# A planned instruction order that counts longer landing times for transfers and a shorter hop from TensorE

## The chip, the cores and the metric

The kernel runs on one core of a Trainium2 chip. The metric is the device time of one execution in microseconds (us); the times below are the median of the runs and their range. The core has five engines. Four matter here: TensorE (PE, matrix products), VectorE (DVE) and ScalarE (ACT, both elementwise work), and SyncE (SP), whose queue issues the transfers (DMAs). Each engine runs its own list of instructions in the order in which it was written, and waits on semaphores for the others.

## The reference

Attention over channels, then two feed-forward layers, on 6016 tokens of 256 channels:

```python
qn = q / (norm(q, axis=1) + 1e-6);  kn = k / (norm(k, axis=1) + 1e-6)
a = softmax(kn.T @ qn / tau)                    # 256 x 256
x = v @ a                                       # 6016 x 256
xn = x / sqrt(mean(x * x, -1) + 1e-6) * rms_g
y = (silu(xn @ w_gate) * (xn @ w_val)) @ w_out  # d_ff 1536
h = y @ w_in2
out = (h - tanh(h)) @ w_out2                    # d_ff 2048
```

## The kernel before

Everything is in fp32 accuracy: each operand of a large product is split into a high part (made by ACT, names ending in `h`) and a low part (made by DVE, names ending in `l`), and one product is three matmuls (`prod`, line 399). Activations are held transposed, channels on partitions, in blocks of 512 tokens. Two blocks make a pair, and there are six pairs; the first is smaller.

The work comes in stages. First the attention matrix, from `q` and `k`, while the weights of the first layer are loaded and converted (`convert`, nine blocks `items`, in the order `gv0`, `w10`, `gv1`, `gv2`, ...). Then pair 0 of the first layer, in plain form. Then pairs 1 to 5 of the first layer: a product of two blocks of weights by two blocks of channels and tokens is done by a scheme with seven products in place of eight (`unit`), on four PSUM banks X, T, Y, Z; its operands B11, B21, B22 and T1 to T4 are parts of the blocks, their sums and differences, which `operands` makes. Each of the six units of a pair is a gate part (tiles `Xg`, `Yg`, ...) and a value part (`Xv`, ...; in `value_sum` DVE makes the sum `c`), and its four results are split (`uc`, `ulc`) and pushed as products into four accumulator banks (`acc`). When an accumulator is full, ACT copies it to `r`, a ring of one buffer (`rr`), and `to_y` writes it to memory. Last come the six pairs of the second layer, eight units each (tiles `Xh`, `Yh`, `Zh`, `Th`; results `wc`), whose sums go out as `outT`.

While a pair of the first layer runs, `x_thread` (line 874) prepares the next one: it multiplies `v` by the attention matrix, then sends the mean squares through memory to turn them (transfers `row`, then `narmp`), takes the inverse root on DVE, writes it (`back`), and reads it spread over all partitions (`rs`, 256 KB each); DVE multiplies `x_0g` and `x_1g` by `rs`, and `operands` follows. Beside it `second_weights` converts the weights of the second layer: load `raw` (512 KB), convert on ACT and DVE to `y`, write it (`l<-y`, `l20s<-y`, ..., 256 KB).

The order of all of this is not that of the program text. Each operation is put into a graph with an engine, a cost, and what it reads and writes (`Graph.op`). `Graph.run` (line 149) is a list scheduler: it plays the four engines in time, and gives each, when it is free, the ready operation of lowest rank. PE ranks by a key, the place of the operation in the program (accumulations get a lag); the others rank by `late`, the latest start that `Graph.latest` (line 226) found by going backward over the last round's order. An operation is ready when the ends of what it depends on, plus a hop between the two engines (`LATENCY`, line 24), have passed. The end of a transfer is counted by its issue, its bytes and a tail (line 33 and lines 189 to 193):

```python
DMA_SETUP, DMA_RATE, DMA_TAIL, DMA_ISSUE = 1000, 385.0, 900, 450
...
                free[e] = t + DMA_ISSUE
                wire = max(t + DMA_SETUP, wire) + o.size / DMA_RATE
                o.end = wire + DMA_TAIL
```

`Graph.schedule` plays six rounds, keeps the order with the earliest end, and the instructions are written in it. The planned times have no other effect: on the chip an instruction waits for its data alone, and those behind it on its engine wait with it.

Of the kernel before, what the change touches and what calls it, by code (L numbers as in the profile page):

```python
# [21 lines left out]


LATENCY = {
    ("PE", "PE"): 0, ("PE", "ACT"): 262, ("PE", "DVE"): 262,
    ("ACT", "PE"): 152, ("DVE", "PE"): 140, ("DVE", "ACT"): 120, ("ACT", "DVE"): 132,
    ("ACT", "ACT"): 130, ("DVE", "DVE"): 116,
    ("SP", "SP"): 100, ("SP", "PE"): 100, ("SP", "ACT"): 100, ("SP", "DVE"): 100,
# [2 lines left out]
COLD = 7000.0  # L31
PATIENT, HOLD, TOLERANCE = ("ACT", "DVE"), 600.0, 60.0
DMA_SETUP, DMA_RATE, DMA_TAIL, DMA_ISSUE = 1000, 385.0, 900, 450


class Op:
    __slots__ = ("eng", "cost", "emit", "preds", "succs", "key", "idx", "start", "end", "late",
                 "ready", "left", "size")

    def __init__(self, eng, cost, emit, key, idx, size):  # L40
        self.eng, self.cost, self.emit, self.key, self.idx, self.size = (
            eng, cost, emit, key, idx, size)
        self.preds, self.succs, self.late = {}, [], None


class Part:
# [42 lines left out]
class View:  # L89
# [5 lines left out]
    @property  # L95
    def ap(self):
        return self.f(self.buf.t)
# [14 lines left out]
class Graph:  # L112
# [36 lines left out]
    def run(self):  # L149

        ops = self.ops
        for o in ops:
            o.left, o.ready = len(o.preds), 0.0
        free = dict.fromkeys(("PE", "ACT", "DVE", "SP"), 0.0)
        known = {e: [] for e in free}
        avail = {e: [] for e in free}
        wire = lag = 0.0

        def rank(o):
            return (o.key if o.eng == "PE" else o.idx if o.late is None else o.late, o.idx)  # L160

        for o in ops:
            if not o.left:
                heappush(known[o.eng], (0.0, o.idx))
        order = []
        while len(order) < len(ops):
            best = None
            for e in free:
                if avail[e]:
                    t = free[e]  # L170
                elif known[e]:
                    t = max(free[e], known[e][0][0])
                else:
                    continue
                if best is None or t < best[0]:
                    best = t, e
            t, e = best
            while known[e] and known[e][0][0] <= t:
                o = ops[heappop(known[e])[1]]
                heappush(avail[e], (*rank(o), o))  # L180
            o = heappop(avail[e])[2]
            if e in PATIENT and o.late is not None:
                o = self.patient(o, t, known[e], avail[e], ops, lag)
                if not isinstance(o, Op):
                    free[e] = o
                    continue
            o.start = t
            if e == "PE" and o.late is not None:
                lag = t - o.late
            if e == "SP":  # L190
                free[e] = t + DMA_ISSUE
                wire = max(t + DMA_SETUP, wire) + o.size / DMA_RATE
                o.end = wire + DMA_TAIL
            else:
                o.end = free[e] = t + o.cost * (2 if e == "PE" and t < COLD else 1)
            order.append(o)
            for s, data in o.succs:
                s.left -= 1
                s.ready = max(s.ready, o.end + self.gap(o, s, data))
                if not s.left:  # L200
                    heappush(known[s.eng], (s.ready, s.idx))
        return order
# [23 lines left out]
    def latest(self, order):  # L226

        end = max(o.end for o in order)
        after = None
        for o in reversed(order):  # L230
            late = end
            for s, data in o.succs:
                late = min(late, s.late - self.gap(o, s, data))
            if o.eng == "PE":
                if after is not None:
                    late = min(late, after.late)
                after = o
            o.late = late - (DMA_SETUP + o.size / DMA_RATE + DMA_TAIL if o.eng == "SP" else o.cost)

    def schedule(self, rounds):  # L240
        for o in self.ops:
# [32 lines left out]
def attn_moe_kernel(  # L274
# [40 lines left out]
    late = []  # L315

    g = Graph()
    slots, early_users = {}, []
# [71 lines left out]
    def lo_of(out, in_, hi, n):  # L390
        return dve(
            lambda: nc.vector.tensor_sub(out=ap(out), in0=ap(in_), in1=f32(ap(hi))), n, 2,  # L392
            [in_, hi], [out])

    def dma(out, in_, size, reads=(), writes=()):
        return g.op(
            "SP", DMA_ISSUE, lambda: nc.sync.dma_start(out=ap(out), in_=ap(in_)), reads, writes,
            size=size)

    def prod(out, w, x, n, start, key=None):  # L400

        (wh, wl), (xh, xl) = w, x

        def emit():
            o = ap(out)
            for i, (a, b) in enumerate(((wh, xh), (wl, xh), (wh, xl))):
                nc.tensor.matmul(  # L407
                    o, ap(a), ap(b), start=start and i == 0, stop=i == 2, skip_group_check=True)

        return g.op("PE", 3 * (n / 2.4 + 13.7), emit, [wh, wl, xh, xl], [out], key=key)  # L410
# [73 lines left out]
    items = []  # L484
# [27 lines left out]
    def convert(c):  # L512

        raw = raws(f"{c['nm']}raw")
        share = W // len(c["src"])
        for s, src in enumerate(c["src"]):
            part = raw.part(s)
            dma(raw.view(lambda t, s=s: t[:, s * share:(s + 1) * share, :].rearrange(
                "p (k n) w -> p k (n w)", k=c["rows"])), src, W * P * 8 // len(c["src"]),
                writes=[part])  # L520
        every = list(raw.parts.values())
        y = ys(f"{c['nm']}y")

        def reads(f):
            before = len(g.ops)
            f()
            o = g.ops[before]
            for p in every:
                for w in p.w:
                    o.preds[w] = True  # L530
                p.r.append(o)
                p.buf.users.append(o)

        reads(lambda: rebias(y, raw, W))
        shift(y, W)
        reads(lambda: sign(y, words(raw, 1), W))
        reads(lambda: bits(y, words(raw, 0), W))
        if "saved" in c:
            dma(c["saved"], y, W * P * 4, [y], [c["saved"]])
        h, l = (new(wpool, f"{c['nm']}{x}", f"{c['nm']}{x}", [P, W], F32R) for x in "hl")  # L540
        both = ["S", "R"]
        activation(h, y, AF.Copy, W, writes=[h.part(x) for x in both])
        dve(lambda: nc.vector.tensor_sub(out=ap(l), in0=ap(y), in1=f32(ap(h))), W, 2,
            [y, *(h.part(x) for x in both)], [l.part(x) for x in both])
        c["h"], c["l"] = h, l
# [39 lines left out]
    def first_sums(i):  # L585
        c = gv[i]
        y = new(act, "wraw", f"s{i}", [P, 2, 4 * P])
        dma(y, c["saved"].view(lambda t: t.rearrange("p (x n) -> p x n", x=2)), W * P * 4,
            [c["saved"]], [y])
        block_sums(y, 2 * P)  # L590
        sh, sl = (new_late(f"s{x}{i}", f"s{x}{i}", [P, 2, 3 * P]) for x in "hl")

        def two(b, key=None):
            return b.view(lambda t: t.rearrange("p (x n) -> p x n", x=2)[:, :, :P], key)

        hi_of(sh, y[:, :, P:], 6 * P)
        hi_of(two(c["h"], "S"), y[:, :, :P], 2 * P)
        lo_of(sl, y[:, :, P:], sh, 6 * P)
        lo_of(two(c["l"], "S"), y[:, :, :P], two(c["h"], "S"), 2 * P)
        for x in range(2):  # L600
            def half(b, key):
                return b
            unit1[i][x] = seven_first(c["h"], c["l"], sh, sl, x)
# [515 lines left out]


    attention()
    for c in items:
        convert(c)
    early_users += [o for b in g.ops for o in [b]]

    xs = [[bank(tag, f"x{b}_{c}") for c, tag in enumerate(tags)]
          for b, tags in enumerate((WORK[:2], WORK[2:]))]
# [193 lines left out]
```

## Time and profile before

| | us |
|---|---|
| median of 3 runs | 1144.27 |
| range of the runs | 1143.41 to 1145.62 |
| the profiled execution, its own time | 1147.1 |
| its span, first to last instruction | 1145.3 |
| PE busy | 1125.6 (98%) |
| DVE busy | 817.5 (71%) |
| ACT busy | 694.0 (61%) |
| mean granted clock of PE | 0.995 |

The profile is of one execution. An engine's busy time is the union of its instructions' times; matmuls are pipelined and their ends modelled, so a busy PE is not PE at its peak. The granted clock is the share of PE's full clock. In the rows further down, `Yv<-T4h,gv4h` reads: writes tile Yv from T4h and gv4h, with buffer numbers left out. What stands behind `<-` in square brackets is what ended the idle time in front of that instruction. Where an instruction waits for several things, the profile names the one that came last.

### The profile page before, as it was taken

How to read it: one execution, taken by the hardware profiler on the slowest of the kernel's cores; microseconds unless marked ns; L12 is line 12 of the kernel's file. 1: busy time of each engine (PE TensorE's matmuls, PEld its weight loads, DVE VectorE, ACT ScalarE, POOL GpSimd, SP SyncE). 2: the span in 40 equal slices, each digit the busy share in tenths (PEclk: the TensorE clock that was granted, in tenths of full speed). 3: DMA queues.
4: the chain of work that ended last, by engine and by line, in shares of the span. 5: the costliest groups of instructions: out<-in, count | busy, mean ns of one | idle time of the engine just before them, and what ended most of it. 6: DMA issues, size and time to landing. Idle time of an engine off the chain costs nothing.

```text
span 1145.3 us, 14185 instructions
## 1 busy us (share of the span) xinstructions
PE 1125.6 (98%) x4986; PEld 927.1 (81%) x4986; DVE 817.5 (71%) x1376; ACT 694.0 (61%) x1199; POOL 0.7 (0%) x6
## 2 busy tenths in 40 slices
PE   9899999999999999999999999999999999999998
PEld 8668887777777887888788899888888888888887
DVE  5988777687678557645966786866867767767664
ACT  6665456665655565555665675756756656656654
POOL 0000000000000000000000000000000000000000
PEclk9999999999999999999999999999999999999999
DMA  9845112422331300010121210200200100100001
GB/s 362 304 149 182 56 64 89 120 84 92 100 107 52 120 20 19 28 42 20 42 88 52 72 54 1 70 1 3 72 1 28 47 1 28 38 1 1 37 1 37
DMA packets 41195, 76.74 MB, mean 67 GB/s; under 512 B 6810, under 2 KB 11674, under 8 KB 41124
## 3 DMA queue, kind: packets, MB, share of 16 engines
q1 hardware_dynamic: 40836, 74.79, 19.6%
q10 hardware_dynamic: 288, 1.05, 0.2%
q8 instruction: 39, 0.64, 0.2%
q14 instruction: 32, 0.26, 0.1%
HBM read 54.02 MB, written 21.80 MB: 66 GB/s over the span
## 4 chain that ended last, share of the span: by engine, by line
PE 76%; DVE 11%; DMA 8%; ACT 3%; issue 2%; SPq 0%; DVEq 0%; ACTq 0%
PE acc L407 33%; PE Yh L407 8%; PE Xh L407 6%; PE Yv L407 4%; PE Yg L407 4%; PE Zh L407 3%; PE Th L407 3%; PE Xg L407 3%; PE Xv L407 2%; DMA rs<-back 2%; PE g L407 2%; PE v L407 2%; DVE tc L388 2%; DVE ulc L392 1%; DMA raw<-w_out_in 1%
## 5 line engine op out<-in xcount | busy, mean ns | idle before, releaser
L392 DVE TENSOR_TENSOR ulc<-wc,uc 128x512 fp32r<-128x512 f32 (+1 forms) x192 | 130.2, 679 | 83.8 <-ACT uc L373 81.4
L373 ACT ACTIVATE uc<-wc 128x512 fp32r<-128x512 f32 (+1 forms) x192 | 119.5, 623 | 103.2 <-PE acc L407 91.4
L373 ACT ACTIVATE uc<-tc 128x512 fp32r<-128x512 f32 x120 | 73.4, 628 | 81.4 <-DVE tc L388 81.0
L392 DVE TENSOR_TENSOR ulc<-tc,uc 128x512 fp32r<-128x512 f32 x120 | 78.5, 683 | 2.7 <-ACT uc L373 2.4
L388 DVE TENSOR_TENSOR Zv<-Yv,m5v 128x512 f32<-128x512 f32 x30 | 20.9, 695 | 40.8 <-PE Yv L407 40.7
L388 DVE TENSOR_TENSOR wc<-Xh,wc 128x512 f32<-128x512 f32 (+1 forms) x48 | 32.5, 676 | 18.6 <-ACT wc L373 18.6
L388 DVE TENSOR_TENSOR Zh<-Yh,m5h 128x512 f32<-128x512 f32 (+1 forms) x48 | 32.9, 686 | 17.9 <-ACT m5h L373 16.0
L373 ACT ACTIVATE wc<-Xh 128x512 f32<-128x512 f32 (+1 forms) x48 | 28.2, 587 | 28.7 <-PE Xh L407 28.5
L415 PE MATMUL S<-q,k 128*128 128x256 f32 x188 | 41.8, 381 | 0.5 <-DMA k<-k_in 0.4
L415 PEld LDWEIGHTS S<-q,k 128*128 128x128 f32 x188 | 35.3, 190 | 6.0 <-issue 1.3
L388 DVE TENSOR_TENSOR wc<-Yh,wc 128x512 f32<-128x512 f32 (+1 forms) x48 | 32.6, 678 | 10.3 <-ACT wc L373 10.3
L373 ACT ACTIVATE wc<-Yh 128x512 f32<-128x512 f32 (+1 forms) x48 | 28.2, 586 | 15.2 <-PE Yh L407 14.5
L373 ACT ACTIVATE r<-acc 128x512 f32<-128x512 f32 (+2 forms) x48 | 27.3, 587 | 15.8 <-PE acc L407 11.3
L373 ACT ACTIVATE m5h<-Th 128x512 f32<-128x512 f32 (+1 forms) x48 | 28.2, 588 | 11.5 <-PE Th L407 11.5
L373 ACT ACTIVATE tc<-Xg 128x512 f32<-128x512 f32 x30 | 17.9, 598 | 27.9 <-PE Xg L407 27.7
L373 ACT ACTIVATE Yh<-Xh 128x512 f32<-128x512 f32 (+1 forms) x48 | 27.6, 575 | 11.7 <-PE Xh L407 10.3
L373 ACT ACTIVATE tc<-Zg 128x512 f32<-128x512 f32 x30 | 17.9, 597 | 25.7 <-PE Zg L407 20.2
L388 DVE TENSOR_TENSOR s<-Yh,m5h 128x512 f32<-128x512 f32 (+1 forms) x48 | 32.5, 676 | 0.3 <-PE Yh L407 0.2
L388 DVE TENSOR_TENSOR wc<-s,wc 128x512 f32<-128x512 f32 (+1 forms) x48 | 32.3, 672 | 0.1
L388 DVE TENSOR_TENSOR wc<-Zh,wc 128x512 f32<-128x512 f32 (+1 forms) x48 | 32.2, 672 | 0.0
L388 DVE TENSOR_TENSOR tc<-Yg,m5g 128x512 f32<-128x512 f32 x30 | 20.7, 690 | 16.0 <-PE Yg L407 15.6
L407 PE MATMUL acc<-uc,w11h 128*128 128x512 f32 x80 | 31.4, 393 | 0.0
(911 smaller groups left out, 3496.9 us busy)
## 6 DMA issues: line engine op xcount, KB each, us to landing
q<-q_in SPq DMA_DIRECT2D x11, 512.0 KB, 8.8
vraw<-vT_in SPq DMA_DIRECT2D x11, 512.0 KB, 4.2
y<-r SPq DMA_DIRECT2D x22, 256.0 KB, 2.2
y<-y SPq DMA_DIRECT2D x20, 256.0 KB, 2.6
outT<-r SPq DMA_DIRECT2D x20, 256.0 KB, 2.0
k<-k_in SPq DMA_DIRECT2D x9, 512.0 KB, 10.3
raw<-w_in_in SPq DMA_DIRECT2D x8, 512.0 KB, 4.4
raw<-w_out_in SPq DMA_DIRECT2D x8, 512.0 KB, 3.8
```

The lines of the kernel that those rows point to most:

```text
L373: nc.scalar.activation(out=ap(out), in_=ap(in_), func=func, **{x: ap(a) for x, a in kw.items()})
L388: return dve(lambda: f(out=ap(out), in0=ap(a), in1=ap(b)), n, 2, [a, b], [out])
L392: lambda: nc.vector.tensor_sub(out=ap(out), in0=ap(in_), in1=f32(ap(hi))), n, 2,
L407: nc.tensor.matmul(o, ap(a), ap(b), start=start and i == 0, stop=i == 2, skip_group_check=True)
L415: lambda: nc.tensor.matmul(ap(out), ap(a), ap(b), start=start, stop=stop, **kw),
```

## The change

Three things are changed, all in the planner. The hop from PE to ACT is counted as 210 ns in place of 262, and that from PE to DVE as 205. Each operation has a new field `slack`, added to the counted end of a transfer and taken off its latest start. Transfers get a slack of 2200 ns from the fourth weight block on (`i > 2`) and in all that follows; those of the attention part and of the first three blocks get none. The line with `early_users` is only written differently.

```diff
 LATENCY = {
-    ("PE", "PE"): 0, ("PE", "ACT"): 262, ("PE", "DVE"): 262,
+    ("PE", "PE"): 0, ("PE", "ACT"): 210, ("PE", "DVE"): 205,
...
 DMA_SETUP, DMA_RATE, DMA_TAIL, DMA_ISSUE = 1000, 385.0, 900, 450
+DMA_SLACK = 2200
...
-        self.preds, self.succs, self.late = {}, [], None
+        self.preds, self.succs, self.late, self.slack = {}, [], None, 0
...
-                o.end = wire + DMA_TAIL
+                o.end = wire + DMA_TAIL + o.slack
...
-            o.late = late - (DMA_SETUP + o.size / DMA_RATE + DMA_TAIL if o.eng == "SP" else o.cost)
+            o.late = late - (DMA_SETUP + o.size / DMA_RATE + DMA_TAIL + o.slack if o.eng == "SP" else o.cost)
...
+    slack = [0]
+
     def dma(out, in_, size, reads=(), writes=()):
-        return g.op(
+        o = g.op(
             "SP", DMA_ISSUE, lambda: nc.sync.dma_start(out=ap(out), in_=ap(in_)), reads, writes,
             size=size)
+        o.slack = slack[0]
+        return o
...
     attention()
-    for c in items:
+    for i, c in enumerate(items):
+        slack[0] = DMA_SLACK if i > 2 else 0
         convert(c)
-    early_users += [o for b in g.ops for o in [b]]
+    early_users += g.ops
+    slack[0] = DMA_SLACK
```

## Rows read from the trace of the kernel before

**Rows 1.** The page's first part: busy us, share of span, instructions of each engine.

```profile
PE 1125.6 (98%) x4986; PEld 927.1 (81%) x4986; DVE 817.5 (71%) x1376; ACT 694.0 (61%) x1199; POOL 0.7 (0%) x6
```

**Rows 2.** Windows: stretch, length, busy us of each engine, clock, DMA share, GB/s.

```profile
140.00:675.00 535.00, 526.33 (x2299) 427.38 (x2298) 379.23 (x669) 316.28 (x563) 0.00 (x0) 1.00 0.21 67
675.00:1145.30 470.30, 466.52 (x2084) 390.27 (x2083) 329.48 (x510) 294.71 (x517) 0.00 (x0) 1.00 0.07 23
```

**Rows 3.** Waits of PE in 140 to 560 us: total us, times, longest us.

```profile
PE Yv L407 <- DVE c L388: 5.2, 4, 2.4
PE Yg L407 <- ACT Yg L373: 0.7, 1, 0.7
...
```

**Rows 4.** Timeline of PE: start us, us, instruction, [idle before <- what ended it].

```profile
246.07 0.50 PE L407 MATMUL Yv<-T4h,gv4h 128*128 128x512 f32 x1 [1.41 <-DVE c L388]
...
348.95 0.50 PE L407 MATMUL Yv<-T4h,gv4h 128*128 128x512 f32 x1 [2.43 <-DVE c L388]
```

**Rows 5.** Timeline of DVE ahead of those two stalls of PE.

```profile
243.52 0.69 DVE L388 TENSOR_TENSOR x_0g<-x_0g,rs 128x512 f32<-128x512 f32 x1 [1.53 <-DMA rs<-back]
...
345.55 0.69 DVE L388 TENSOR_TENSOR x_0g<-x_0g,rs 128x512 f32<-128x512 f32 x1 [1.70 <-DMA rs<-back]
...
347.60 0.69 DVE L388 TENSOR_TENSOR x_0g<-x_0g,rs 128x512 f32<-128x512 f32 x1 [0.76 <-DMA rs<-back]
348.21 0.68 DVE L388 TENSOR_TENSOR c<-Yv,m5v 128x512 f32<-128x512 f32 x1
```

**Rows 6.** Waits of DVE and ACT on transfers, 140 to 560 us, as rows 3.

```profile
DVE x_0g L388 <- DMA rs<-back: 14.9, 6, 4.9
...
ACT y L373 <- DMA raw<-w_out_in: 7.7, 6, 3.1
...
ACT r L373 <- DMA y<-r: 3.1, 4, 1.6
...
DVE y L388 <- DMA l<-y: 3.1, 2, 1.6
```

**Rows 7.** DMA issues: transfer, queue, count, KB each, median us from issue to landing.

```profile
y<-r SPq DMA_DIRECT2D x22, 256.0 KB, 2.2
...
raw<-w_in_in SPq DMA_DIRECT2D x8, 512.0 KB, 4.4
...
l<-y SPq DMA_DIRECT2D x16, 256.0 KB, 4.2
rs<-back SPq DMA_DIRECT2D x10, 256.0 KB, 4.1
```

**Rows 8.** A window, as rows 2, just behind the stall that ends at 348.95.

```profile
350.00:354.00 4.00, 4.00 (x13) 3.15 (x12) 3.48 (x7) 3.12 (x6) 0.00 (x0) 0.61 0.01 3
```

**Rows 9.** Timelines of PE and ACT in the second layer, as rows 4.

```profile
849.06 0.39 PE L407 MATMUL Xh<-B11l,l24h 128*128 128x512 f32 x1
849.29 0.39 PE L407 MATMUL acc<-uc,l22h 128*128 128x512 f32 x1
...
849.49 0.58 ACT L373 ACTIVATE Yh<-Xh 128x512 f32<-128x512 f32 x1 [0.28 <-PE Xh L407]
...
851.10 0.39 PE L407 MATMUL Th<-T1l,l2s 128*128 128x512 f32 x1
...
851.59 0.60 ACT L373 ACTIVATE m5h<-Th 128x512 f32<-128x512 f32 x1 [0.34 <-PE Th L407]
```

**Rows 10.** Timeline of ACT: the first and the last of four copies r.

```profile
573.94 0.60 ACT L373 ACTIVATE r<-acc 128x512 f32<-128x512 f32 x1 [2.81 <-PE acc L407]
...
585.17 0.60 ACT L373 ACTIVATE r<-acc 128x512 f32<-128x512 f32 x1 [0.56 <-DMA y<-r]
```

**Rows 11.** A window as rows 2, and timelines of DVE and PE around T4.

```profile
545.00:563.00 18.00, 17.94 (x78) 14.01 (x77) 17.64 (x30) 12.32 (x22) 0.00 (x0) 1.00 0.19 52
...
563.16 0.68 DVE L392 TENSOR_TENSOR T4l<-t,T4h 128x512 fp32r<-128x512 f32 x1
...
568.97 0.39 PE L407 MATMUL Yg<-T4h,gv0h 128*128 128x512 f32 x1
```

More of the change, by code (lines that the diff above doesn't have):

```diff
@@ L33 @@
 DMA_SETUP, DMA_RATE, DMA_TAIL, DMA_ISSUE = 1000, 385.0, 900, 450
+DMA_SLACK = 2200
 class Op:
     __slots__ = ("eng", "cost", "emit", "preds", "succs", "key", "idx", "start", "end", "late",
-                 "ready", "left", "size")
+                 "ready", "left", "size", "slack")
     def __init__(self, eng, cost, emit, key, idx, size):
```

## The prediction

> **What bounds the kernel now.** I read the busy line first. TensorE (PE) is busy 1125.6 of 1145.3 us [rows 1], and none of its products is added or taken away, so all that an order can win lies in the 19.7 us in which it is idle and in time at a low clock. The windows by stage say where that is. From 675 us on PE is busy 466.52 of 470.30 us, and the missing 3.78 us are the tail behind its last product: nothing to win there, only to lose [rows 2]. In 140 to 675 us, the five block pairs of the first layer, it is busy 526.33 of 535 us: 8.67 us idle [rows 2].
>
> Who ends these waits? The table of PE's waits names VectorE (DVE) and ScalarE (ACT), led by the sum `c` in DVE with 5.2 us in 4 waits [rows 3]. No row names a DMA, and it would be wrong to stop there. The two longest, 1.41 us at 246.07 and 2.43 us at 348.95, end with a `c` on DVE [rows 4]. In DVE's own order the `c` of 348.21 stands right behind `x_0g<-x_0g,rs`, for which DVE sat idle 1.70 us and then 0.76 us until the transfer `rs<-back` landed; the stall at 246.07 has the same wait, 1.53 us, ahead of it [rows 5]. So a short instruction that needs late data stands in the written order ahead of one that PE needs. The waits of DVE and ACT on transfers in 140 to 560 us are of this kind: 14.9 us for `rs`, 7.7 us for `raw`, 3.1 us for `y<-r`, 3.1 us for `l<-y` [rows 6].
>
> The planner's own numbers explain it. It counts 1000 + bytes/385 + 900 ns from issue to landing: for 256 KB 1000 + 681 + 900 = 2581 ns, for 512 KB 3262 ns. The profile has 4.1 us for `rs`, 4.2 us for `l<-y` (both 256 KB), 4.4 us for `raw` (512 KB), but 2.2 us for `y<-r` (256 KB) [rows 7]. Three of the four land 1.1 to 1.6 us after the plan has their readers start; the fourth lands early.
>
> After the stall near 349 us the granted clock over 350 to 354 us is 0.61 [rows 8]. Those 4 us did the work of 4 x 0.61 = 2.44 us at the full level, 2.4 GHz; the rest was spent at 1.2 GHz, and 1.56 us were lost.
>
> **The change, part by part.** *Longer landings.* Every transfer from the fourth weight block's load on is counted 2200 ns longer: 256 KB takes 4781 ns in the plan, 512 KB 5462 ns. Both are above the medians of `rs`, `l<-y` and `raw` [rows 7]. The readers then stand behind other work of their engine, and the wait in front of `c` goes. No instruction is added; what moves is the place of the readers (10 products `x_0g`, 10 `x_1g`, the splits behind them, the conversions of the second layer's weights), and of the transfers on the SP queue, which go out earlier where the plan now counts a chain as longer. Worth: all 8.67 us [rows 2] if every stall of 140 to 675 us has such a transfer behind it, plus the 1.56 us of clock [rows 8], together 10.2 us. The lower end is nothing, if the readers keep their places. I take the upper end less 1.2 us. The rows show the cause for the two longest stalls alone, 3.84 us with the clock loss beside it [rows 4, 8]; for the rest I go by 28.8 us of engine waits on transfers, 14.9 + 7.7 + 3.1 + 3.1, in the same stretch [rows 6]. The 1.2 us is held back for crowding, below.
>
> One rule speaks against this part, and stands here by itself. The Trainium skill, "DMA: Bandwidth & Descriptors", section "Anatomy of one DMA", gives one transfer about 2.0 us and its bytes at 436 GB/s, fitted for another issuing path; for 256 KB that is an estimate of 2.60 us, the plan's old count. `y<-r` agrees with its 2.2 us, `rs` and `l<-y` with 4.1 and 4.2 us do not [rows 7]. By the rule this part would win nothing.
>
> *What the longer count puts late.* The chain `row`, `narmp`, `back`, `rs` is four transfers in series, so the plan may place `x_0g` up to 4 x 2.2 = 8.8 us later. Behind it come the splits of eight operands. In 545 to 563 us, the last such stretch, DVE is busy 17.64 of 18 us, and `T4l`, one of the last of them, starts at 563.16 us, 5.8 us before PE reads T4 at 568.97 us [rows 11]. So the cover is 5.8 us, less than 8.8. But the backward pass counts the longer landings too, which makes the square roots ahead of `back` more urgent, and the reader's true data is not later. I take 0.25 us for each of five such chains, the 1.2 us above; without cover it would be 8.8 - 5.8 = 3 us each, 15 us.
>
> *The single buffer for results.* `r` lives in a ring of one (`rr`): each of the four copies that end a pair waits for the transfer of the one before. The plan's least spacing was 0.49 + 0.25 + 2.58 + 0.10 = 3.42 us and becomes 5.62 us. Measured, the first and the fourth copy start at 573.94 and 585.17 us, 11.23 us apart [rows 10]; three new spacings are 16.9 us, so the fourth accumulator bank comes free 5.6 us later. At nothing, while PE has other products to take: that is the cover (the next unit's products, which the ring of split operands lets run ahead one unit). Without it, up to 5.6 us at each of six pair ends.
>
> *The shorter hop.* The plan lets ACT or DVE start 210 or 205 ns after a product instead of 262. A product is three matmuls 0.23 us apart, and the plan's end is 0.23 us after the last one's start. `Yh<-Xh` starts at 849.49 us, 0.43 us after the last matmul of Xh at 849.06: a hop of 0.20 us, the new number. `m5h<-Th` starts at 851.59 us, 0.49 us after that of Th at 851.10: a hop of 0.26 us, the old number [rows 9]. So the new plan is right for one kind and 0.05 us too early for the other. It can win nothing where PE is busy throughout. It loses where a product stands exactly at its operand's planned time: nothing if none does, 0.05 us in each of 78 units (30 of the first layer, 48 of the second) if one in each does, 3.9 us. Products come 0.68 us apart, so with some three such operands in a unit the chance is about 3 x 0.05 / 0.68 = 0.22; I take 0.22 x 3.9 = 0.9 us.
>
> *The head, up to 140 us.* No slack in the attention part and the first three weight blocks. The order may shift by a fraction of a microsecond; I take nothing, plus or minus 1 us.
>
> **Sum.** 8.67 + 1.56 - 1.2 - 0.9 = 8.1 us. The profiled execution, 1147.1 us with a span of 1145.3, would be 1139.0 us; it is 2.8 us above the median of the runs, 1144.27, from which the same 8.1 us give 1136.2.
>
> **The rivals.** *Crowding (B).* The operand chain moves later into a full DVE and half of the gain comes back as new PE waits at the pair starts: 1 us for each of five chains instead of 0.25, 3.8 us more, 1140.0. For it: 17.64 of 18 us [rows 11]. Against: the 5.8 us of cover. At 1.9 us each the gain is gone.
>
> *No effect (C).* The change doesn't do what it says: a reader's rank moves with its transfer's, so the same neighbours stand around it and PE waits as now: 1144.3, give or take 1.5. By the rule of the Trainium skill above the time would be this one too. Against: the plan never starts a reader before the counted landing, which is now 2.2 us later, so DVE must be given other work or be idle in the plan.
>
> *The ring of one (D), slower.* Landings of `y<-r` are over-counted by 4.78 - 2.2 = 2.6 us, and the order holds accumulators back at six pair ends. With half of the 5.6 us uncovered: 6 x 2.8 = 16.8 us lost, 1136.2 + 16.8 = 1153.0; it decides from 8.1 / 6 = 1.35 us a pair end. For it: ACT already waits 3.1 us for `y<-r` [rows 6]. Against: the real transfer is not slower, and PE has products of the next unit.
>
> *The tight hop (E), slower.* All three operands of a unit stand at their planned time, in all 78 units: 3 x 3.9 = 11.7 us in place of 0.9, 1136.2 + 10.8 = 1147.0. Against: list order is not that regular.
>
> **How the numbers follow.** Forecast 0.57 (1134 to 1139.5), B 0.18 (1139.5 to 1142), C 0.12 (1142 to 1146.5), D 0.08, E 0.05. The predicted time is the forecast's, 1136.2. The low end, 1133.5, is the full 10.2 us with some of the head's 1 us; the high end, 1143.5, takes in B and part of C: about 0.55 + 0.18 + 0.07 = 0.8. About 0.2% (2.3 us) is what a measurement of this kernel can tell from no change: faster than 1142.0 has the forecast and B with 0.75, within 0.2% C with 0.12, slower D and E with 0.13.
>
> **What would show it.** Right: PE busy in 140 to 675 us rises in share, DVE's wait for `rs` falls from 14.9 us to under 4, no stretch at the low clock behind 140 us, the second layer still without waits. Crowding would show as PE waiting for operands (T3, T4, B22) at pair starts; D as PE waiting for ACT's `r`, with the four copies some 5.6 us apart; E as many PE waits under 0.1 us behind 675 us; C as the same wait for `rs`. The prediction is wrong if the readers stay where they are, or if a new order costs PE over 6 us in places that have none now.

## The result and the profile after

| | before | changed |
|---|---|---|
| median, us | 1144.94 (1143.41 to 1146.51) | 1133.85 (1133.30 to 1135.77) |
| ratio to before, 95% interval | | 0.9906 [0.9887, 0.9925] |
| profiled execution, its own time and span, us | 1147.1, 1145.3 | 1133.97, 1132.2 |

The changed kernel is 11.1 us faster. The forecast was 8.1 us less than before, with 1133.5 to 1143.5 us as the range.

The busy line and the windows by stage of the changed kernel (columns as in rows 1 and 2):

```profile
PE 1122.2 (99%) x4986; PEld 926.7 (82%) x4986; DVE 818.5 (72%) x1376; ACT 694.6 (61%) x1199; POOL 0.7 (0%) x6
...
140.00:675.00 535.00, 534.64 (x2353) 436.81 (x2352) 386.64 (x682) 323.67 (x578) 0.00 (x0) 1.00 0.21 67
675.00:1132.20 457.20, 453.39 (x2019) 378.29 (x2017) 320.41 (x494) 286.59 (x501) 0.00 (x0) 1.00 0.07 23
```

In 140 to 675 us TensorE is idle for 0.36 us where it was 8.67 [rows 2], and no stretch at the low clock is left there: the one at 0.61 [rows 8] is gone. The tail is the same 3.8 us. So 8.31 + 1.56 = 9.9 us went where the prediction looked.

VectorE's timeline around the last of the five chains, where it had waited in front of `x_0g`:

```profile
526.42 0.70 DVE L389 TENSOR_TENSOR Zv<-Yv,m5v 128x512 f32<-128x512 f32 x1 [3.17 <-PE Yv L412]
...
528.42 0.69 DVE L389 TENSOR_TENSOR c<-Yv,m5v 128x512 f32<-128x512 f32 x1 [0.69 <-PE Yv L412]
...
532.88 0.69 DVE L389 TENSOR_TENSOR x_0g<-x_0g,rs 128x512 f32<-128x512 f32 x1
```

What answers to [rows 5] is the order: `c` now stands ahead of `x_0g`, and VectorE waits for TensorE (3.17 us) and no longer for `rs`. The transfer itself is no faster; its landing times over the whole execution, from the answer on the tile `rs`:

```profile
DMA to landing us min/median/max: 3.9/4.1/4.3
```

Of the waits on transfers in 140 to 560 us [rows 6] two are left, 0.2 us and this one:

```profile
ACT y L374 <- DMA l26s<-y: 0.8, 1, 0.8
```

The first and the last of the four copies `r` of a pair end, from ScalarE's timeline:

```profile
266.05 0.60 ACT L374 ACTIVATE r<-acc 128x512 f32<-128x512 f32 x1 [2.45 <-PE acc L412]
...
282.96 0.65 ACT L374 ACTIVATE r<-acc 128x512 f32<-128x512 f32 x1
```

They span 16.9 us in place of 11.2 [rows 10], as worked out for the ring of one (15.2 to 18.8 us at the six pair ends), and TensorE is busy through it.

The two profiled spans differ by 13.1 us. Part of the rest is in the head, in which nothing was expected. Up to 140 us TensorE is idle for 5.9 us in place of 7.3 (1.4 us less), and it runs less long at 1.2 GHz behind the softmax. The window 50 to 62 us, first of the kernel before, then of the changed one:

```profile
50.00:62.00 12.00, 8.77 (x18) 4.42 (x19) 10.64 (x22) 6.72 (x13) 0.00 (x0) 0.72 0.46 156
```

```profile
50.00:62.00 12.00, 8.58 (x26) 4.56 (x27) 9.56 (x22) 6.75 (x13) 0.00 (x0) 0.86 0.56 181
```

That is 12 x (0.28 - 0.14) = 1.7 us. It is one execution of each kernel, and whether the change brings it is open: e1 below, which has the same slack, has 0.72 in that window, as before.

```profile
50.00:62.00 12.00, 8.51 (x18) 4.33 (x19) 9.64 (x22) 5.88 (x12) 0.00 (x0) 0.72 0.55 175
```

8.31 + 1.56 + 1.4 + 1.7 = 13.0 us looks like the whole difference, but that is chance. Two matmuls that stand at the same place of the program in every kernel, the first of pairs 1 to 5 (`Xg`) and the first of the second layer (`Xh`), divide it better. First the kernel before, then the changed one:

```profile
163.59 0.40 PE L407 MATMUL Xg<-B11h,gv0h 128*128 128x512 f32 x1
653.85 0.36 PE L407 MATMUL Xh<-B11h,l20h 128*128 128x448 f32 x1
```

```profile
160.36 0.40 PE L412 MATMUL Xg<-B11h,gv0h 128*128 128x512 f32 x1
638.72 0.37 PE L412 MATMUL Xh<-B11h,l20h 128*128 128x448 f32 x1
```

The head is 3.2 us shorter. The pairs take 478.36 us in place of 490.26, 11.9 us less, which is 2.0 more than the 9.9 us of idle time and low clock. The second layer, from `Xh` to the end of the span, takes 493.5 us in place of 491.5: 2.0 us are lost there, which the runs don't place. So far the forecast looks right and a little short. The experiments show that it was two errors that nearly cancelled.

### The profile page after: what moved, and what is told of

Its sections match the earlier page's. It is cut to its first block, busy times and chain, and to the rows that moved or that the text cites. A ratio compares the mean times of both kernels' runs of the same rounds, so it can differ in the third digit from the quotient of the medians.

```text
span 1132.2 us, 14182 instructions
## 1 busy us (share of the span) xinstructions
PE 1122.2 (99%) x4986; PEld 926.7 (82%) x4986; DVE 818.5 (72%) x1376; ACT 694.6 (61%) x1199; POOL 0.7 (0%) x6
## 4 chain that ended last, share of the span: by engine, by line
PE 95%; DMA 2%; DVE 2%; issue 1%; ACT 0%; DVEq 0%; ACTq 0%
PE acc L412 40%; PE Yh L412 9%; PE Yv L412 6%; PE Xh L412 6%; PE Yg L412 6%; PE Xg L412 4%; PE Xv L412 4%; PE Th L412 3%; PE Zh L412 3%; PE g L412 3%; PE v L412 3%; PE x L412 2%; PE Tv L412 2%; PE Tg L412 2%; PE Zv L412 2%; PE Zg L412 2%
## 5 line engine op out<-in xcount | busy, mean ns | idle before, releaser
L389 DVE TENSOR_TENSOR Zv<-Yv,m5v 128x512 f32<-128x512 f32 x30 | 20.9, 697 | 49.6 <-PE Yv L412 49.5
L374 ACT ACTIVATE wc<-Yh 128x512 f32<-128x512 f32 (+1 forms) x48 | 28.2, 588 | 15.2 <-PE Yh L412 14.0
L374 ACT ACTIVATE m5h<-Th 128x512 f32<-128x512 f32 (+1 forms) x48 | 28.3, 589 | 15.0 <-PE Th L412 11.2
L374 ACT ACTIVATE r<-acc 128x512 f32<-128x512 f32 (+2 forms) x48 | 27.4, 590 | 11.2 <-PE acc L412 10.8
L374 ACT ACTIVATE tc<-Zg 128x512 f32<-128x512 f32 x30 | 17.9, 597 | 23.2 <-PE Zg L412 16.8
L412 PE MATMUL acc<-uc,w10h 128*128 128x512 f32 x80 | 31.2, 390 | 0.0
```

The lines of the kernel that those rows point to most:

```text
L374: nc.scalar.activation(out=ap(out), in_=ap(in_), func=func, **{x: ap(a) for x, a in kw.items()})
L389: return dve(lambda: f(out=ap(out), in0=ap(a), in1=ap(b)), n, 2, [a, b], [out])
L412: nc.tensor.matmul(o, ap(a), ap(b), start=start and i == 0, stop=i == 2, skip_group_check=True)
```

## The experiments

Each ratio is to the kernel before, run on the same chip. The runs were on several chips, on which the median of the kernel before went from 1144.94 to 1147.26 us, so kernels of different groups (e1 to e4, e5 to e8, e9 to e12) are compared by ratio. All experiments start from the changed kernel; their diffs are against it.

| run | hop to ACT, DVE (ns) | slack (ns) | median, us | ratio [95%] | PE idle 140 to 675 |
|---|---|---|---|---|---|
| changed kernel | 210, 205 | 2200 | 1133.85 | 0.9906 [0.9887, 0.9925] | 0.36 |
| e1 | 262, 262 | 2200 | 1129.30 | 0.9854 [0.9839, 0.9870] | 0.42 |
| e2 | 210, 205 | 0 | 1145.02 | 0.9989 [0.9979, 0.9998] | 6.63 |
| e3 | 262, 262 | 2200, mean-square chain alone | 1137.51 | 0.9925 [0.9911, 0.9939] | 3.81 |
| e4 | 262, 262 | 2200, all but that chain | 1133.71 | 0.9893 [0.9877, 0.9909] | 3.79 |
| e5 | 210, 262 | 2200 | 1132.83 | 0.9872 [0.9852, 0.9892] | 0.55 |
| e6 | 262, 205 | 2200 | 1131.37 | 0.9861 [0.9841, 0.9881] | 0.62 |
| e7 | 105, 103 | 2200 | 1136.41 | 0.9906 [0.9888, 0.9925] | 0.51 |
| e8 | 320, 320 | 2200 | 1128.11 | 0.9837 [0.9816, 0.9859] | 0.41 |
| e9 | 262, 262 | 1100 | 1130.09 | 0.9853 [0.9837, 0.9870] | 0.18 |
| e10 | 262, 262 | 4400 | 1135.13 | 0.9894 [0.9879, 0.9909] | 1.91 |
| e11 | 262, 262 | 2200, none for `r` | 1128.96 | 0.9843 [0.9828, 0.9858] | 0.17 |
| e12 | 420, 420 | 2200 | 1130.22 | 0.9852 [0.9838, 0.9867] | 1.98 |

### The two halves apart (e1, e2)

```diff
-    ("PE", "PE"): 0, ("PE", "ACT"): 210, ("PE", "DVE"): 205,      # e1
+    ("PE", "PE"): 0, ("PE", "ACT"): 262, ("PE", "DVE"): 262,
...
-DMA_SLACK = 2200                                                  # e2
+DMA_SLACK = 0
```

> The longer landing count of the changed kernel, with the old hop of 262 ns. Theory A (the gain is the late transfers, the hop is worth nothing): 1133 to 1136 us, PE idle in 140 to 675 us under 1 us, no wait of DVE or ACT on rs. Rival B (the shorter hop brings part of it, since products are planned where their operands really are): 1137 us or more, with PE waits in the pairs of the first layer. Rival C (any other order would have got rid of the stalls by chance): anywhere in 1133 to 1145 us, with stalls whose releasers are not transfers.

> The shorter hop of the changed kernel, with no slack on any transfer. Theory A: 1143 to 1147 us, DVE still idle 12 us or more in front of x_0g for the transfer rs, PE idle 7 to 10 us in 140 to 675 us. Rival B (the hop carries part of the gain): 1141 us or less. Rival C (chance order): anywhere, with the waits for rs gone or not.

The longer landing count alone is worth 16.8 us (1146.06 to 1129.30), more than the whole change. The shorter hop alone is worth 1.0 us, just clear of nothing. Put on top of the slack it costs: 1133.85 against 1129.30 us, or 0.9906 against 0.9854 of before, which is 4.5 to 6 us. The two intervals don't overlap. e1 lies under A's 1133 to 1136 us: A was right on the transfers and took the hop for worth nothing, which it is not. B is refuted.

With no slack TensorE's idle time stays, and it is still transfers that the other engines wait for, though others. In 140 to 560 us of e2:

```profile
DVE y L389 <- DMA l<-y: 12.4, 4, 4.0
ACT y L374 <- DMA raw<-w_out_in: 9.5, 5, 3.5
...
DVE x_0g L389 <- DMA rs<-back: 2.6, 4, 1.1
```

I had expected 12 us or more for `rs`; it is 2.6, and `l<-y` has taken its place. Which late transfer an engine is caught by depends on the order; in this order, too, it is caught by one. C needs an order free of such stalls without the slack, and this one has them.

### Which transfers (e3, e4)

```diff
+    def dma_x(*a):                  # e3: slack for row, narmp, back and rs alone
+        o = dma(*a)                 # e4: the same four with o.slack = 0, all others as changed
+        o.slack = DMA_SLACK
+        return o
```

Both have the old hop, and in e3 the two assignments to `slack[0]` are 0.

> Old hop, slack of 2200 ns on the four transfers of the mean-square chain alone (row, narmp, back, rs). Theory A in its part for this chain: the stalls of before that have a wait for rs in front of them (those ending at 144.38, 246.07, 348.95, 445.92 and 543.44 us, 0.38 + 1.41 + 2.43 + 0.17 + 0.18 = 4.6 us) and the 1.6 us of low clock go, 6.2 us: 1138 to 1140 us; the waits for raw and for the writes of converted weights stay. Rival D (only the weights' transfers matter, since the one at 246.07 has l<-y in front of it as well): 1142 us or more.

> Old hop, slack of 2200 ns on every transfer of the changed kernel but the four of the mean-square chain. Theory A: the rest of the stalls goes, 8.3 - 4.6 = 3.7 us, and up to 1.2 us of idle time in the head: 1139 to 1142 us, with DVE still idle 12 us or more for rs. Rival D (only the weights' transfers matter): 1136 us or less.

e3 gained 8.6 us and e4 12.4 us, both more than the stalls that I had listed for them, 6.2 and at most 4.9 us. In time e4 lies where rival D wanted it, but D's reason fails with e3: the chain matters too. What each leaves behind in 140 to 560 us fits the theory. First e3:

```profile
DVE y L389 <- DMA l<-y: 12.0, 4, 3.9
ACT y L374 <- DMA raw<-w_in_in: 6.3, 3, 4.4
```

and e4, where 12 us or more had been expected for `rs`:

```profile
DVE x_0g L389 <- DMA rs<-back: 9.2, 3, 4.9
```

The two gains add to 20.9 us, 4.1 more than both parts give together. The low clock near 349 us is gone in either profile, which counts 1.6 us twice. The rest would be stalls that needed either wait gone, as the one at 246.07 with its two; that is argued, not shown.

### Where the hop's cost hides

TensorE is idle for 0.36 us in the changed kernel and 0.42 us in e1, and yet e1 is 4.5 us faster. The window of e1 to set beside that of the changed kernel above:

```profile
140.00:675.00 535.00, 534.58 (x2379) 442.82 (x2378) 390.40 (x689) 329.53 (x585) 0.00 (x0) 1.00 0.22 68
```

As busy, but 2379 matmuls in place of 2353. The same two matmuls as above, in e1:

```profile
162.03 0.40 PE L412 MATMUL Xg<-B11h,gv0h 128*128 128x512 f32 x1
635.68 0.36 PE L412 MATMUL Xh<-B11h,l20h 128*128 128x448 f32 x1
```

The pairs take 473.65 us here and 478.36 in the changed kernel, 4.7 us more for the same products. Something slows TensorE while its busy time is full. The waits of its weight loads (PEld) in that window show what, first in the changed kernel, then in e1, then in the kernel before:

```profile
PEld Yv L412 <- ACT Yv L374: 6.2, 15, 0.5
PEld Yg L412 <- ACT Yg L374: 1.5, 6, 0.3
```

```profile
PEld Yv L412 <- ACT Yv L374: 1.1, 4, 0.5
PEld Yg L412 <- DVE Zg L389: 1.1, 6, 0.2
```

```profile
PEld Yv L407 <- DVE c L388: 9.1, 9, 2.9
PEld Yv L407 <- DVE Zv L388: 4.1, 9, 0.6
```

15 of the 30 value units of the changed kernel wait at one place, the product `Yv<-T2` behind ScalarE's copy `Yv<-Xv`. One of them, on TensorE's timeline and ScalarE's in the changed kernel:

```profile
569.17 0.39 PE L412 MATMUL Yg<-T4l,gv1h 128*128 128x512 f32 x1
...
570.53 0.39 PE L412 MATMUL acc<-ulc,w10h 128*128 128x512 f32 x1
570.92 0.50 PE L412 MATMUL Yv<-T2h,sh 128*128 128x512 f32 x1
571.26 0.39 PE L412 MATMUL Yv<-T2h,sl 128*128 128x512 f32 x1
...
569.66 0.60 ACT L374 ACTIVATE tc<-Yg 128x512 f32<-128x512 f32 x1 [0.30 <-PE Yg L412]
570.29 0.58 ACT L374 ACTIVATE Yv<-Xv 128x512 f32<-128x512 f32 x1
```

The matmul behind 570.53 was due at 570.76. The copy ends at 570.87, and the matmul starts at 570.92, 0.16 us late. No idle time is shown, since the record of the matmul before it ends at 570.92 as well: a record lasts 0.39 us, and the next matmul is due after 0.23. The matmul behind the stall then takes 0.34 us to the next, 0.11 more than usual. So this wait costs 0.27 us and shows as next to nothing in the idle time.

Why is the copy late? Between the last matmul of `Yg` (569.17) and `Yv<-T2` stand six matmuls, two products of accumulation. In e1 there are nine, three products, behind the same instructions of ScalarE at the same distance:

```profile
567.19 0.39 PE L412 MATMUL Yg<-T4l,gv1h 128*128 128x512 f32 x1
...
569.23 0.39 PE L412 MATMUL acc<-ulc,w10h 128*128 128x512 f32 x1
569.45 0.39 PE L412 MATMUL Yv<-T2h,sh 128*128 128x512 f32 x1
...
567.67 0.60 ACT L374 ACTIVATE tc<-Yg 128x512 f32<-128x512 f32 x1 [0.30 <-PE Yg L412]
568.30 0.58 ACT L374 ACTIVATE Yv<-Xv 128x512 f32<-128x512 f32 x1
```

The plan's own numbers give the step. From the end of `Yg` it counts the hop, two copies of 512 / 1.2 + 60 = 487 ns (`act_cost`) and 152 ns back to TensorE: 1.336 us with a hop of 210 ns, 1.388 with 262. Two products count 1.362 us, so they cover the first and not the second, and a third is placed. On the chip the way took 1.52 us (569.40 to 570.92): two products are too few, three enough. The hop is only 0.05 us of the error; the two copies, counted at 0.97 us, took 1.21 (569.66 to 570.87), and the way back, counted at 0.15 us, took 0.05. The traces bear the step out: of the 17 units in which `Yg` stands in front of the accumulations, the changed kernel has two products in 14, and all 14 start late; it has three in the other three, and e1 in all 17, and none of these does. The 14 stalls cost 0.21 to 0.28 us each, 3.5 us together, of the 4.7 us. (The 15th wait, of the first unit, is in e1 too.) That counting the copies longer would serve as well as the longer hop follows from this sum, but no run has it.

The kernel before had such hidden waits as well, behind late sums `c` and `Zv` of VectorE, and e1 lost them: its pairs are 16.6 us shorter, of which idle time (8.25) and low clock (1.56) are 9.8.

### The hop, from half to double (e5 to e8, e12)

```diff
-    ("PE", "PE"): 0, ("PE", "ACT"): 210, ("PE", "DVE"): 205,
+    ("PE", "PE"): 0, ("PE", "ACT"): 210, ("PE", "DVE"): 262,      # e5
+    ("PE", "PE"): 0, ("PE", "ACT"): 262, ("PE", "DVE"): 205,      # e6
+    ("PE", "PE"): 0, ("PE", "ACT"): 105, ("PE", "DVE"): 103,      # e7
+    ("PE", "PE"): 0, ("PE", "ACT"): 320, ("PE", "DVE"): 320,      # e8
+    ("PE", "PE"): 0, ("PE", "ACT"): 420, ("PE", "DVE"): 420,      # e12
```

> Slack as in the changed kernel, the hop from TensorE to ScalarE 210 ns, that to VectorE left at 262. Theory F (the shorter hop costs the changed kernel 4 to 5 us, because ScalarE's copy Yv<-Xv reaches the product Yv<-T2 0.27 us after TensorE is ready for it, in 15 of the 30 value units): the waits of the weight loads of Yv on ScalarE's Yv are back at about 6 us, 1132 to 1135 us. Rival G (the 4 us belong to the one order that these two numbers gave, not to the hop to ScalarE): 1128 to 1131 us.

> Slack as in the changed kernel, the hop from TensorE to VectorE 205 ns, that to ScalarE left at 262. Theory F: no wait on ScalarE's Yv over 2 us in sum, 1128 to 1131 us. Rival G: anywhere in 1128 to 1136 us, with other products that wait.

> Slack as in the changed kernel, both hops at half of its value (105 and 103 ns), so 0.1 to 0.16 us under what the trace shows. Theory F (a hop that is counted too short puts products where their operands are not there yet, and the loss grows with the error): 1137 us or more, with many waits of TensorE's weight loads on ScalarE and VectorE, in the second layer too. Rival G: no more than the changed kernel, 1129 to 1136 us.

> Slack as in the changed kernel, both hops at 320 ns, longer than any the trace shows. Theory F (a hop counted too long costs nothing while TensorE has other products): 1127 to 1130 us, waits of the weight loads on ScalarE and VectorE in the first layer's pairs no more than with 262. Rival H (a longer hop holds the units back and TensorE runs out of products): 1132 us or more.

> Slack as in the changed kernel, both hops at 420 ns. Theory F (margin is free as long as TensorE has other products, and the gain ends once no product meets a late operand): 1126 to 1129 us, the rest of the hidden waits gone. Rival H (a longer hop holds the units back): 1130 us or more.

The waits of the weight loads on `Yv` in 140 to 675 us, in e5, e6, e7 and e8:

```profile
PEld Yv L412 <- ACT Yv L374: 6.4, 15, 0.7
```

```profile
PEld Yv L412 <- ACT Yv L374: 1.7, 4, 0.5
```

```profile
PEld Yv L412 <- ACT Yv L374: 7.7, 18, 0.5
```

```profile
PEld Yv L412 <- ACT Yv L374: 0.5, 1, 0.5
```

The wait belongs to the hop to ScalarE: with that at 210 ns or less it is there 15 to 18 times (changed kernel, e2, e5, e7), with 262 or more at most 5 times (the kernel before and the other nine). What it costs is read from the pairs, in the one profiled execution of each:

| run | hop to ACT, DVE (ns) | first `Xg` to first `Xh`, us | more than e1 | waits of `Yv` on the copy |
|---|---|---|---|---|
| e1 | 262, 262 | 473.65 | | 4 |
| changed | 210, 205 | 478.36 | 4.7 | 15 |
| e5 | 210, 262 | 477.48 | 3.8 | 15 |
| e6 | 262, 205 | 475.81 | 2.2 | 4 |
| e7 | 105, 103 | 479.67 | 6.0 | 18 |
| e8 | 320, 320 | 472.94 | -0.7 | 1 |

The shorter hop to ScalarE alone brings 3.8 us, that to VectorE alone 2.2 us, which I didn't place. By ratio e1, e5 and e6 can't be told apart (intervals overlapping). The times of e5 and e6 fell on theory F's side or near it, e5 in its range, e6 0.4 us above it. Half the hop (e7) has a few more waits: the loss doesn't grow in proportion, and the time, 1136.41 us, lies between F's 1137 and G's 1136. That fits the step, for which 105 and 210 ns are the same. The shorter hop is not a loss by itself: without the slack (e2) the same 15 waits are there, 6.5 us, and that kernel is no slower than before. With 320 ns (e8) the waits are all but gone, and the ratio is the lowest, 0.9837, but not clear of e1's or of that with 420 ns. With 420 ns TensorE has idle time that shows, 1.98 us; its longest wait in e12 in that window:

```profile
PE Yh L412 <- DVE Zh L389: 0.8, 1, 0.8
```

So margin shows no cost up to 320 ns here, and at 420 the idle time of rival H begins; its time of 1130 us or more was met by 0.2 us, and the ratio, 0.9852, is that of e1.

### The size of the slack and the ring of one (e9 to e11)

```diff
-DMA_SLACK = 2200
+DMA_SLACK = 1100                                # e9
+DMA_SLACK = 4400                                # e10
...
-            dma(y.view(lambda a: a[m * P:(m + 1) * P, :]), r, ...)     # e11, and the same for outT
+            dma_x(y.view(lambda a: a[m * P:(m + 1) * P, :]), r, ...)   # o.slack = 0
```

All three have the old hop, so they stand beside e1.

> Old hop of 262 ns, slack of 1100 ns in place of 2200: 256 KB counts as 3.7 us and 512 KB as 4.4 us, under or about the medians of 4.1 to 4.4 us that the trace of before shows. Theory A (what is left is the landing beyond the count): a few waits of 0.3 to 1 us on rs, raw and l<-y return, 1130 to 1135 us. Rival I (any count above the old one is enough, since the rest is covered by other work): 1128 to 1130 us.

> Old hop of 262 ns, slack of 4400 ns, double. The four copies r of a pair end are then counted 0.49 + 0.25 + 6.98 + 0.1 = 7.8 us apart, 23.5 us for three, and the mean-square chain 17.6 us longer than in before. Theory J (the cover gives out: crowding of the operands, and the ring of one result buffer): PE idle in 140 to 675 us 3 us or more, 1133 us or more. Rival K (the cover is larger than I took it): 1128 to 1131 us, PE idle under 1 us.

> Old hop of 262 ns, slack of 2200 ns on all but the results that leave through r (y<-r and outT<-r), which land in 2.0 to 2.8 us and were counted rightly. Theory J (over-counting them holds accumulators back): copies r again 3.5 to 4.5 us apart and 1 us or more faster than with slack on all, under 1128.3 us. Rival K (products of the next unit cover it): the copies move together, the time stays within 1128 to 1131 us.

With half the slack waits on transfers return, as theory A wanted. In 140 to 675 us of e9:

```profile
ACT y L374 <- DMA raw<-w_out_in: 3.5, 3, 2.4
ACT y L374 <- DMA l25s<-y: 2.7, 1, 2.7
```

But they cost nothing that shows: TensorE has no wait there, and the ratio is that of e1. The time, 1130.09 us, lies on the border of both ranges; by the ratio rival I was right. A late transfer hurt only where an operand of TensorE stood behind it.

With double the slack the cover gives out: 1135.13 us, 0.9894 against 0.9854. The first and the last of four copies `r` in e10 are 25.2 us apart (16.9 in the changed kernel):

```profile
265.56 0.58 ACT L374 ACTIVATE r<-acc 128x512 f32<-128x512 f32 x1
...
290.77 0.59 ACT L374 ACTIVATE r<-acc 128x512 f32<-128x512 f32 x1
```

J's time came, its 3 us of idle time didn't: 1.91 us show. More is hidden as above (its pairs take 477.90 us, 4.2 more than in e1), with 2356 matmuls in the window where e1 has 2379:

```profile
140.00:675.00 535.00, 533.09 (x2356) 437.18 (x2355) 387.00 (x684) 321.88 (x576) 0.00 (x0) 1.00 0.22 68
...
PEld Yv L412 <- DVE Zv L389: 2.7, 6, 0.6
PEld Yv L412 <- ACT Yv L374: 2.6, 5, 1.0
...
PEld acc L412 <- ACT r L374: 0.9, 2, 0.5
```

The waits are spread. That on `r` is 0.9 us, so crowding is the likelier of J's two reasons; the runs don't separate them.

In e11 the copies moved together again, as this first and last of four show (11.0 us apart), and the time did not move beyond what can be told from e1 (0.9843 against 0.9854, intervals overlapping):

```profile
265.93 0.60 ACT L374 ACTIVATE r<-acc 128x512 f32<-128x512 f32 x1 [2.81 <-PE acc L417]
...
276.95 0.60 ACT L374 ACTIVATE r<-acc 128x512 f32<-128x512 f32 x1
```

With a slack of 2200 ns the ring of one costs nothing that shows: K.

## Why the prediction was right, and where it was not

*The bound.* Here a step failed: "all that an order can win lies in the 19.7 us in which it is idle and in time at a low clock". TensorE also loses time while it counts as busy, 0.27 us in the stall shown above. The bound taken for the pairs, 8.67 + 1.56 = 10.2 us, was passed: e1 won 16.6 us there, of which the idle time (8.67 - 0.42 = 8.25) and the low clock (1.56) are 9.8. The other 6.8 us are hidden time, since the pairs hold the same products; the head of e1 gave 1.6 us (163.59 to 162.03), and its second layer lost 0.9.

*Longer landings.* Mechanism, place and cause were right: readers moved behind other work, the waits for `rs` went from 14.9 us to none, and no transfer got faster. The term was mis-sized, 10.2 less 1.2, so 9.0 us, against 16.8 measured alone. The 1.2 us kept back for crowding were not needed at 2200 ns; e10 shows that they would have been at 4400. Two readings were off, without harm to the sum. At a mean clock of 0.61 about 3.1 of the 4 us were at 1.2 GHz, not 1.56; the loss of 1.56 us is right. And the cover of 5.8 us was measured to the read of T4h; `T4l` itself ends at 563.84 us and is read at 569.43, 5.6 us later.

*The rule of the Trainium skill* in "DMA: Bandwidth & Descriptors" (section "Anatomy of one DMA"), by which this part would win nothing, doesn't hold for these transfers, whose issuing path is another than the one it was fitted for: the landing of `rs` stayed at 3.9 to 4.3 us against the rule's estimate of 2.60, and counting it and the others longer gained 16.8 us.

*The ring of one.* Right: the spacing worked out, 16.9 us, is about the one measured (15.2 to 18.8), and without it (e11) no time is won that shows, so other products cover it.

*The shorter hop.* Right in kind and mis-sized: 0.9 us forecast, 4.5 to 6 measured. Three operands a unit that each meet the error of 0.05 us with a chance of 0.07 was the wrong picture. Products are placed whole, 0.68 us each, so the shorter hop took one product away in front of `Yv<-T2` in 14 units, and there the product started 0.16 us late in the unit shown, mostly because the two copies of ScalarE were counted short, and the stall cost 0.27. Rival E had "all three operands of a unit [...] in all 78 units", 11.7 us; the truth lay between.

*The head and the second layer.* Nothing was forecast for either. The profiled executions differ by 1.4 us of idle time and 1.7 us of clock in the head, and the second layer, in which the prediction saw only something to lose, lost 2.0 us.

*The sum.* 9.0 - 0.9 = 8.1 us forecast; 16.8 less about 5 measured. Both terms were too small, the gain by 7.8 and the loss by about 4, and so the total was only 3 us short. That the time, 1133.85 us, lies 0.35 us inside the range is luck in its size, not in its direction.

## What to carry to other kernels

In an order that is planned ahead, count a transfer at about what its slow kind takes (here 4.1 us; 3.7 and 4.8 us counted for 256 KB gave the same time, 2.6 cost 16.8 us, and 7.0 cost some 5): a reader planned too early holds up everything behind it on its engine, and one planned too late costs nothing while there is other work. The hop between engines is one term of a sum: 210 ns, which fits one kind of copy, lost to 262, because the hop that mattered took 0.26 us and the copies behind it were counted short, for which the longer hop had made up in part. So hold the whole way from one product to the next against the trace, not one term of it, and vary the margin; a slack of 4400 ns loses again. Before idle time is taken for all that can be won, compare the time between two fixed instructions, and look at the waits of the weight loads.

## What the hardware showed that I had not expected

A stall of TensorE up to 0.16 us leaves no idle time in the trace, because a record of a 512-column matmul lasts 0.39 us and the next starts 0.23 us after it; and the first matmul behind such a stall takes 0.11 us more than the others (a record of 0.50 us). 14 such stalls were 3.5 us of the changed kernel.

Behind the same wait of 3.0 us for the softmax, TensorE's low clock of 1.2 GHz cost 3.4 us in the profiled execution of the kernel before (12 x 0.28) and 1.7 us in that of the changed one (12 x 0.14); in e1 it cost 3.4 again. What decides between the two the runs don't tell.
